# Local attention and two expert layers: larger loads for the mixed units, one load for the coarse values, a mask product in four tiles, and a new order

## The chip, the cores and the metric

The kernel runs on one core of one Trainium2 chip. The metric is the time of one execution on the device, in microseconds (us). Engines: PE is TensorE's matmul, PEld its weight load, DVE is VectorE, ACT is ScalarE, POOL is GpSimd, SP is SyncE, which here only issues DMAs.

## The reference

Three stages follow each other, all in float32 outside and at float32's precision inside.

- Attention: 2 batches, 8 heads, 576 positions, head size 64. Each position attends to the 7 positions at a distance under 4 (the local part). Beside it queries, keys and values are averaged over groups of four positions, 144 groups attend to all 144, and each result is repeated four times (the coarse part). The two results are added.
- First expert layer: h = x @ w_in with x of 1152 tokens x 512, w_in 512 x 2048; g = P(h)/Q(h), P a cubic with coefficients a, Q made of |h|, h squared and b; then g @ w_out back to 512.
- Second expert layer: the same shapes with g = h * tanh(log(1 + exp(h))).

The weights arrive as 64-bit words and are taken apart on the chip.

## The kernel before, in words

**Attention in units.** Heads are taken in pairs; 64-row halves of a tile hold the two heads of a pair. A unit is four windows of 64 queries. Kinds 0 and 1 are the four windows of one pair (tokens 0 to 255 and 256 to 511 of a batch). Kind 2 is the mixed unit: the last 64 tokens of all four pairs at once. There are 18 units, two of them mixed. prep() fetches and turns the keys of a pair, and sums its coarse values: load() at lines 551 to 561, vload() at 605 to 609 (a load of 64 rows and one of 8), then two additions at 615 and 619 on GpSimd or VectorE. unit() does one unit: qload() fetches queries (643; four loads in a mixed unit), vload() fetches window values (658; four loads, eight in a mixed unit), pe_a() transposes queries (546), pe_b() computes scores: first a product of eye2 and mask puts the mask in PSUM (702), then the local scores (709) and the coarse ones (717) are added on tiles of 64 rows by 32 columns. Maxima, exponentials and sums follow on VectorE and ScalarE, pe_d() transposes the weights (786, 791), pe_e() forms the coarse products (816) and the local ones (826).

**Expert layers.** A weight grain (256 columns of w_in or 256 rows of w_out) is fetched by load() at 983 and 988, and turned into a high and a low part by ScalarE and VectorE (lines 1000 to 1031). Each product is three: high x high, high x low, low x high (1144 and 1277 in the first layer; 1458, 1514 and 1279 in the second). In the second layer some products use seven in place of eight block products, with additions on VectorE (1480) between them, and sums() (1307 on) forms their inputs.

**Order.** Nothing runs in the order of the code. Each piece is a task with engines, an estimated cost, a due time (prio), buffers it takes and uses, and tasks it must follow. Plan.run() (114) walks through estimated time and issues on every engine the ready task with the smallest due time. It keeps an estimate of DMA too: up to 8 loads on their way, each with an issue time and a moving time. The due times are made from a step's place in the expert layers and constants: LEAD (attention ahead of its products), LLEAD and CLEAD (fetching and converting weights), LOFF, KOFF, VOFF, VROFF (loads of queries, keys, window values, coarse values against their unit), UOFF (one number per unit), GOFF (one per weight grain), SUMS. Where TensorE would have nothing, fill() puts in a product of a blank tile (line 527). All DMAs go out on SP's queue. Buffers of attention lie in one tile, "att", among them three places for queries, two for window values and one for coarse values, with more places in "wrk" for the first token group.

Of the kernel before, what the change touches and what calls it, by code (L numbers as in the profile page):

```python
# [12 lines left out]
BF16 = mybir.dt.bfloat16  # L13
# [7 lines left out]
NEG = -1.0e9  # L21
# [2 lines left out]
EDGE, LEAST = 2.0 ** -60, 1e-30  # L24


SECOND = 1.8
COLD, FILL_ALL = 3.4, 20
WINDOW, FILL, FILL_END = 3.4, 0.9, 450.0
LEAD, CLEAD, LLEAD, OLAG = 38, 14, 40, 18  # L30
PROL, PSTEP, VOFF, VROFF, LOFF, KOFF = -45, 2.5, 2, -1, 7, 9
GROUPS = ([6, 6, 4], [4, 4, 4, 4])
KCUT, MIX = 4, (1, 4)
MKP = -45
NKN, NVW, NXT, NQN = 2, 2, 3, 3
XVR, XQN, XVW = 2, 0, 0
SUMS = 5
NRAW, NWT, NRING, NRING2 = 2, 2, 3, (2, 1)
LAT = {"pe": 0.2, "act": 0.16, "dve": 0.15, "pool": 0.15, "sp": 1.1}
QUEUED = 8  # L40
UOFF = [-3.0, 0.0, 0.0, 3.0, 4.5, 3.0, 3.0, -1.5, 6.0, 0.0, 0.0, -4.5, -4.5, 4.5, 6.0, 4.5, -1.5, -1.5]
GOFF = [0.0, 0.0, 0.0, 0.0, -4.0, -4.0, -10.0, -6.0, 2.0, -4.0, 10.0, 12.0]
HP = 15


# [34 lines left out]
class Plan:  # L80
# [33 lines left out]
    def run(self, names):  # L114
# [79 lines left out]
        while True:  # L194
            for e in names:
# [3 lines left out]
                while ready[e]:  # L199
                    item = heapq.heappop(ready[e])  # L200
                    t = item[2]
                    if t.started:
                        continue
                    one = next(iter(t.engs))
                    if e != one and until[one] + t.engs[one] <= now + t.engs[e] + SECOND:
                        held.append(item)
                        continue
                    if not place(t, e):
                        held.append(item)
                        continue  # L210
                    t.started = True
                    t.fn(e) if len(t.engs) > 1 else t.fn()
                    begin = max(now, 0.65) if e == "sp" else now
                    if e == "pool" or e == "dve" and t.port:

                        begin = max(now, port[0])
                        port[0] = begin + t.engs[e]
                    end = until[e] = begin + t.engs[e] * (2 if e == "pe" and now < COLD else 1)
                    there = end + LAT[e]
                    if t.dma:  # L220
                        end = begin
                        for issue, move in t.dma:
                            end = max(end, landed[-QUEUED]) + issue
                            moved = max(moved, end + 0.3) + move
                            landed.append(moved + LAT["sp"])
                        until[e], there = end, landed[-1]
                    n += 1
                    heapq.heappush(events, (end, n, 0, e, t))
                    heapq.heappush(events, (there, n, 1, e, t))
                    for k in banks(t):  # L230
                        touched.setdefault(k, {})[e] = there
                    if t.next is not None:
                        t.next.deps -= 1
                        if not t.next.deps:
# [38 lines left out]
def kernel(  # L273
# [31 lines left out]


    ident = const.tile([128, 128], F32, name="ident")
    eye2 = const.tile([128, 128], BF16, name="eye2")
    mask = const.tile([128, 11, WK], BF16, name="mask")
    band = const.tile([64, 92], BF16, name="band")  # L310
# [54 lines left out]
    kn_s = lay("att", NKN, 768, parts=96)  # L365
    vr_s = lay("att", 1, 1024, (4, 4, D), parts=72)
    qn_s = lay("att", NQN, 256)
    vw_s = lay("att", NVW, 512, (4, 2, D), parts=64 + WK)
    s_s = lay("att", 2, 256, (4, 64))
    pd_s = lay("att", 2, SD)  # L370
# [78 lines left out]


    def bands():
        nc.gpsimd.affine_select(
            out=band, in_=band, compare_op=ALU.is_ge, fill=NEG, base=-8, pattern=[[1, 92]], channel_multiplier=-1,
        )
        nc.gpsimd.affine_select(
            out=band, in_=band, compare_op=ALU.is_ge, fill=NEG, base=14, pattern=[[-1, 92]], channel_multiplier=1,
        )

    def masks(kind, w, n):
        for b in range(2):  # L460
            h = slice(HB * b, HB * b + HB)
            lo = window(kind, w, b) - 64 * w + 11
            m0 = MASK0[kind] + (SLOT[w] if kind == 0 else 0)
            nc.vector.tensor_copy(
# [6 lines left out]

    def eyes():
        for h in range(2):
            nc.vector.tensor_copy(out=eye2[:64, 64 * h:64 * h + 64], in_=ident[:64, :64])
# [11 lines left out]
    def under():  # L486
        nc.vector.memset(eye2[64:], 0.0)
        nc.vector.memset(mask[64:], 0.0)

    t_m = add({"dve": 0.1}, lambda: nc.vector.memset(band, 0.0), -1900)  # L490
    t_un = add({"dve": 0.4}, under, -880)
    t_cd = add({"dve": 0.6}, zeros, -1000)
    t_bn = add({"pool": 0.5}, bands, -900, after=[t_m])
    t_mk = [
        add({"dve": 0.2 + 0.05 * len(ws)}, lambda x=(i, ws): [masks(x[0], *w) for w in x[1]], (-890, MKP, MKP)[i], after=[t_bn])
        for i, ws in enumerate((((0, 1), (1, 1), (2, 1), (3, 1)), ((4, 4),), ((8, 4),)))
    ]
# [50 lines left out]
    def prep(bb, p, prio, slots, start):  # L548
# [62 lines left out]
        m0 = add({"sp": 1.25}, vload, prio + VROFF, take=[vr], chain="vr", dma=[(0.65, 0.8), (0.6, 0.12)])  # L611

        def va(e):
            tv = vr.v
# [14 lines left out]
    def unit(u, slots, start):  # L629
# [4 lines left out]
        qn, vw, qp, qT, qx = Buf(qn_s + xq), Buf(vw_s + xv), Buf(slots["q"]), Buf(qT_s), Buf(qx_s)  # L634
        sc, pt, po, px = Buf(slots["s"]), Buf(slots["pt"]), Buf(slots["po"]), Buf(px_s)
        tm, s, pd, pT, od, xt = Buf(tm_s), Buf(s_s), Buf(pd_s), Buf(pT_s), Buf(od_s), Buf(xt_s)
        mix = [qx] if mixed else []

        def qload():
            for i, p in enumerate(pairs):  # L640
                w, m = wins[i][1], n // len(pairs)
                src = q[bb, 2 * p:2 * p + 2, 64 * w:64 * w + 2 * m, :]
                nc.sync.dma_start(  # L643
                    out=qn.v[m * i:m * i + m].rearrange("p (r h d) -> p r h d", h=2, d=D),
                    in_=src.rearrange("h (p r) d -> p r h d", r=2),
                )

        l0 = add({"sp": 0.65}, qload, prio - LOFF, take=[qn], chain="ld", dma=[(0.65, 0.24)] * 4 if mixed else [(0.65, 0.58)])

        m0 = MASK0[kind]  # L650
        keys = [(p, [window(kind, w, b) for b in range(2)]) for p, w in wins]

        def vload():
            for w0, nb in ((0, 4), (2, 4)) if not mixed else [(w, 2) for w in range(4)]:
                p, (k0, k1) = keys[w0]
                for hh in range(2):
                    src = v[bb, 2 * p + hh]
                    nc.sync.dma_start(
                        out=vw.v[64 * (w0 // 2):64 * (w0 // 2) + WK, 2 * (w0 % 2):2 * (w0 % 2) + nb, hh, :],
                        in_=bass.AP(src.tensor, src.offset + k0 * D, [[D, WK], [(k1 - k0) * D, nb], [1, D]]),  # L660
                    )

        vl = add({"sp": 1.0}, vload, prio + VOFF, take=[vw], chain="vw", dma=[(0.45, 0.11)] * 8 if mixed else [(0.45, 0.33)] * 4)

        def pe_a():
            q2 = qp.v[:, :2 * n].rearrange("c (p r) -> c p r", r=2)
            for r in range(2):
                flip(q2[:, :, r], qn.v, r, n)
# [30 lines left out]
        def pe_b():  # L699

            hs = [slice(0, 64), slice(64, 128)]
            nc.tensor.matmul(
                sc.v[:, :nw * WK], eye2, mask[:, m0:m0 + nw].rearrange("p w x -> p (w x)"), start=True, stop=False,
            )
            for w in range(nw):
                for b in range(2):
                    for h in hs:
# [12 lines left out]
                        )  # L720

        tb = add(
            {"pe": 1.6 if mixed else 0.86}, pe_b, prio,
            after=tq + [kv_done[p] for p in pairs] + [t_i16, t_un, t_mk[kind]],
            take=[sc, tm, s, pd],
            use=[qT] + mix, chain="pb",
        )
# [81 lines left out]
        def pe_e():  # L809
# [10 lines left out]
            for m in range(2):  # L820
                for b in range(2):
                    for hh in range(2):
                        for a in range(2):
                            h, r = hs[hh ^ a], slice(64 * a, 64 * a + WK)
                            c = 128 * m + h.start + HB * b
                            nc.tensor.matmul(  # L826
                                px.v[h, a, 64 * m + HB * b:64 * m + HB * b + HB], vw.v[r, 2 * m + b, hh ^ a, :],
                                pT.v[r, c:c + HB], start=True, stop=True,
                            )

# [603 lines left out]
    def seven(st):  # L1434
# [42 lines left out]
        def plus(dst, i, src, after, and_=None):  # L1477
# [96 lines left out]
```

## Time and profile before

| what | value |
|---|---|
| median of 3 runs | 482.44 us (480.46 to 484.45) |
| the profiled execution | 482.31 us, of which 480.4 us are the span from the first to the last instruction |
| granted TensorE clock | 0.998 |
| PE busy | 469.4 us, 98% |
| PEld busy | 429.1 us, 89% |
| DVE busy | 377.0 us, 78% |
| ACT busy | 338.3 us, 70% |
| POOL busy | 57.1 us, 12% |
| moved by DMA | 47.18 MB in 45981 packets, 30576 of them under 512 B |

Busy time is the time in which at least one instruction of the engine runs. Matmuls overlap, so a sum of their durations is more than the time they take on the engine. "Idle before" is the time an engine stood still before an instruction, with what released it. SPq is the queue of SP, in which a DMA's issue takes the time shown.

### The profile page before, as it was taken

What the parts mean: (1) busy time and instruction counts of PE and PEld (TensorE: products, weight loads), DVE (VectorE), ACT (ScalarE), POOL (GpSimd) and SP (SyncE); (2) the same over time, 40 slices, a digit from 0 to 9 for tenths busy, and PEclk for the clock granted to TensorE, in tenths of its full rate; (3) what the DMA queues carried; (4) which work ended last, traced back from release to release, by engine and by line L of the source; (5) the groups of instructions that cost most, each with busy time, mean ns of one, the idle gap of its engine ahead of it and who ended that gap; (6) DMA issues with size and microseconds to landing.
All of it is one profiled execution on the core that took longest, in us unless ns stands there. A gap on an engine that the chain in (4) does not pass through costs nothing.

```text
span 480.4 us, 9823 instructions
## 1 busy us (share of the span) xinstructions
PE 469.4 (98%) x4052; PEld 429.1 (89%) x4052; DVE 377.0 (78%) x565; ACT 338.3 (70%) x529; POOL 57.1 (12%) x80
## 2 busy tenths in 40 slices
PE   8998999999999999999999999999999999999996
PEld 4667888889999999999999999898989898989885
DVE  6677999899899968997998999988596669524342
ACT  5678898786889799998879797578666446422320
POOL 2644434563000000000000000000000000000000
PEclk9999999999999999999999999999999999999999
DMA  9878887611522312343022022134304220000103
GB/s 170 196 178 198 243 200 188 166 37 35 176 89 88 123 54 89 96 125 131 0 89 88 1 88 89 39 111 146 143 15 162 87 89 1 1 0 0 67 0 132
DMA packets 45981, 47.18 MB, mean 98 GB/s; under 512 B 30576, under 2 KB 31344, under 8 KB 45936
## 3 DMA queue, kind: packets, MB, share of 16 engines
q1 hardware_dynamic: 45936, 46.54, 33.7%
q8 instruction: 32, 0.52, 0.5%
q14 instruction: 13, 0.11, 0.1%
HBM read 44.17 MB, written 2.36 MB: 97 GB/s over the span
## 4 chain that ended last, share of the span: by engine, by line
PE 73%; DVE 13%; DMA 8%; ACT 3%; SPq 2%; issue 1%; ACTq 0%
PE psum L1279 19%; PE psum L1144 18%; PE psum L1277 15%; PE psum L1458 11%; PE psum L1514 5%; DMA att<-in_q_dram 3%; DMA raw<-in_moe_w_in_dram 3%; DVE wt L1014 1%; PE psum L826 1%; DMA att<-in_v_dram 1%; DVE xl L1300 1%; PE psum L546 1%; SPq L643 1%; DVE wrk L1318 1%; DVE wo L1031 1%
## 5 line engine op out<-in xcount | busy, mean ns | idle before, releaser
L1144 PE MATMUL psum<-xh,wi 128*128 128x384 f32 (+1 forms) x336 | 83.4, 319 | 0.2 <-DVE wrk L1173 0.2
L1277 PE MATMUL psum<-gg,wo 128*128 128x384 f32 (+1 forms) x480 | 76.3, 313 | 0.0
L1277 PEld LDWEIGHTS psum<-gg,wo 128*128 128x128 f32 x480 | 72.8, 189 | 0.4 <-issue 0.2
L1144 PEld LDWEIGHTS psum<-xh,wi 128*128 128x128 f32 x336 | 59.1, 189 | 1.4 <-issue 0.9
L1144 PE MATMUL psum<-xl,wi 128*128 128x384 f32 (+1 forms) x168 | 52.4, 312 | 0.0
L1279 PE MATMUL psum<-wo,gg 128*128 128x512 f32 x216 | 51.7, 391 | 0.0
L1279 PE MATMUL psum<-wo,late_g 128*128 128x512 f32 x216 | 51.3, 391 | 0.0
L1279 PEld LDWEIGHTS psum<-wo,late_g 128*128 128x128 f32 x216 | 40.4, 188 | 8.0
L1279 PEld LDWEIGHTS psum<-wo,gg 128*128 128x128 f32 x216 | 40.4, 188 | 7.9
L1014 DVE SCALAR_TENSOR_TENSOR wt<-wt,raw 128x1024 int32<-128x1024 int32 x32 | 40.0, 1252 | 6.8 <-ACT wt L1000 6.5
L1000 ACT ACTIVATE wt<-raw 128x1024 f32<-128x1024 f32 x32 | 36.5, 1140 | 10.9 <-DVE wo L1031 4.8
L1007 ACT ACTIVATE raw<-raw 128x1024 int32<-128x1024 uint16 x32 | 36.7, 1147 | 5.1 <-DMA raw<-in_moe_w_out_dram 3.4
L1514 PE MATMUL psum<-xh,wi 128*128 128x384 f32 x128 | 34.5, 335 | 0.0
L1144 PEld LDWEIGHTS psum<-xl,wi 128*128 128x128 f32 x168 | 31.8, 189 | 0.0
L1390 DVE TENSOR_TENSOR part<-psum,part 128x512 f32<-128x512 f32 x27 | 17.8, 687 | 13.7 <-PE psum L1279 13.7
L1144 PE MATMUL psum<-xh,late_r 128*128 128x384 f32 x96 | 25.5, 334 | 0.0
L527 PE MATMUL psum<-blank 128*128 128x480 bf16 x86 | 22.9, 390 | 1.2 <-DVE band L490 1.2
L1031 DVE TENSOR_TENSOR wo<-wt,wo 128x1024 fp32r<-128x1024 f32 x14 | 17.1, 1219 | 8.7 <-ACT wo L1026 8.7
L1026 ACT ACTIVATE wo<-wt 128x1024 fp32r<-128x1024 f32 x11 | 11.7, 1062 | 17.1 <-DVE wt L1020 7.7
L1514 PEld LDWEIGHTS psum<-xh,wi 128*128 128x128 f32 x128 | 23.3, 188 | 0.2
L1164 ACT ACTIVATE wrk<-psum 128x768 f32<-128x768 f32 (+1 forms) x27 | 19.8, 734 | 5.1 <-PE psum L1144 4.8
L1088 ACT ACT_TABLE_LOAD x17 | 21.8, 1283 | 0.3
(165 smaller groups left out, 1043.5 us busy)
## 6 DMA issues: line engine op xcount, KB each, us to landing
raw<-in_moe_w_in_dram SPq DMA_DIRECT2D x16, 1024.0 KB, 6.0
raw<-in_moe_w_out_dram SPq DMA_DIRECT2D x16, 1024.0 KB
att<-in_v_dram SPq DMA_DIRECT2D x64, 48.0 KB, 4.0
out_dram<-part SPq DMA_DIRECT2D x9, 256.0 KB, 2.1
att<-in_q_dram SPq DMA_DIRECT2D x16, 128.0 KB, 4.2
att<-in_k_dram SPq DMA_DIRECT2D x6, 288.0 KB, 4.5
att<-in_v_dram SPq DMA_DIRECT2D x6, 256.0 KB, 5.7
wrk<-in_k_dram SPq DMA_DIRECT2D x2, 288.0 KB
```

Of the source, the lines that this page charges most:

```text
L527: nc.tensor.matmul(view[:, :480], blank[:, :128], blank, start=True, stop=True)
L1000: nc.scalar.activation(out=t.v, in_=words(r)[:, :, 1].bitcast(F32), func=AF.Prelu if fold else AF.Identity, scale=2.0 ** -112, **({"alpha" ...
L1007: nc.scalar.activation(out=words(r)[:, :, 0], in_=r.v.bitcast(U16).rearrange("p (n four) -> p n four", four=4)[:, :, 1], func=AF.Copy, sca ...
L1014: nc.vector.scalar_tensor_tensor(out=ti, in0=ti, scalar=3, in1=words(r)[:, :, 0], op0=ALU.logical_shift_left, op1=ALU.bitwise_or)
L1031: ENG[e].tensor_tensor(out=w.v[:, 1], in0=s.v, in1=w.v[:, 0].bitcast(F32), op=ALU.subtract)
L1088: nc.scalar.preload_act_table_set(name)
L1144: nc.tensor.matmul(st.h.v[:, i, :T], w.v[:, ww, ks], xx[:, kk, c0:c0 + T], start=(nn == 0 and (st.big or i == 0)), stop=(nn == 3 * KD - 1 ...
L1164: nc.scalar.activation(out=vw(st.a), in_=H(), func=AF.Square)
L1277: nc.tensor.matmul(A(d)[:, :T], w.v[:, ww, lo + d * 128:lo + (d + 1) * 128], vw(gg)[:, i, :], start=start, stop=stop)
L1279: nc.tensor.matmul(A(d), vw(gg)[:, i, sl], w.v[:, ww, lo:lo + DM], start=start, stop=stop)
L1458: nc.tensor.matmul(dst.v[:, :TW], wv.v[:, ww, at:at + 128], x(h, kk), start=bool(take) and nn == 0, stop=nn == 5, skip_group_check=not take,)
L1514: nc.tensor.matmul(h.v[:, i, :TW], w.v[:, ww, at:at + 128], xx[:, kk, c0:c0 + TW], start=nn == 0, stop=nn == 3 * KD - 1)
```

## The change

- A mixed unit fetches its queries in one load of 64 rows by 8 heads (it was four loads), into a place of 512 columns that covers the last two of the three query places, and transposes four blocks of 64 rows in place of two of 128. Its window values come in four loads of four windows (eight of two), with another order of the windows in the tile.
- Coarse values come in one load of 72 rows.
- The mask product becomes four, on tiles of 64 rows by 32 columns; so eye2 has 64 columns on both halves, band and mask are filled on all 128 rows, and the two memsets of the lower halves go.
- The loads of a and b go out on ScalarE's queue, ahead of everything else there.
- The planner adds 0.8 us to its estimate of DMA for each 7 us that DMA moves (FETCH: packets that bring instructions).
- Constants of the order change; plus() of the second layer gets a due time earlier by HP.

```diff
-SECOND = 1.8
+SECOND = 1.6
-LEAD, CLEAD, LLEAD, OLAG = 38, 14, 40, 18
-PROL, PSTEP, VOFF, VROFF, LOFF, KOFF = -45, 2.5, 2, -1, 7, 9
+LEAD, CLEAD, LLEAD, OLAG = 38, 20, 30, 22
+PROL, PSTEP, VOFF, VROFF, LOFF, KOFF = -45, 2.5, 2, 2, 5, 9
-SUMS = 5
+SUMS = 20
-UOFF = [-3.0, 0.0, 0.0, 3.0, 4.5, 3.0, 3.0, -1.5, 6.0, 0.0, 0.0, -4.5, -4.5, 4.5, 6.0, 4.5, -1.5, -1.5]
-GOFF = [0.0, 0.0, 0.0, 0.0, -4.0, -4.0, -10.0, -6.0, 2.0, -4.0, 10.0, 12.0]
+FETCH = (0.8, 7.0)
+UOFF = [1.5, 0.0, 1.5, 12.0, 13.5, 13.5, 9.0, 18.0, 12.0, 9.0, -3.0, -6.0, -1.5, -3.0, 7.5, 10.5, -1.5, -9.0]
+GOFF = [0.0, 2.0, 0.0, 2.0, -4.0, -4.0, -4.0, -20.0, 18.0, 0.0, -6.0, 22.0]
...
-                            moved = max(moved, end + 0.3) + move
+                            first = max(moved, end + 0.3)
+                            moved = first + move + FETCH[0] * (int((first + move) / FETCH[1]) - int(first / FETCH[1]))
...
+    qm_s = [Place("att", qn_s[-2].lo, 512, (8, D), 64)]
...
-        for b in range(2):
-            h = slice(HB * b, HB * b + HB)
+        for r0 in range(0, 128, HB):
+            b, h = r0 // HB % 2, slice(r0, r0 + HB)
...
-        nc.sync.dma_start(out=a_sb, in_=a.partition_broadcast(128))
-        nc.sync.dma_start(out=b_sb, in_=b.partition_broadcast(128))
+        nc.scalar.dma_start(out=a_sb, in_=a.partition_broadcast(128))
+        nc.scalar.dma_start(out=b_sb, in_=b.partition_broadcast(128))
...
-    t_ab = add({"sp": 0.9}, c_sp, -34, dma=[(0.65, 0.1), (0.5, 0.1)])
+    t_ab = add({"act": 1.15}, c_sp, -2000, dma=[(0.65, 0.1), (0.5, 0.1)])
...
-            for lo, hi in ((0, 64), (64, 72)):
-                nc.sync.dma_start(out=dst[lo:hi], in_=src[lo:hi])
+            nc.sync.dma_start(out=dst, in_=src)
...
+            if mixed:
+                nc.sync.dma_start(out=qn.v, in_=q[bb, :, 64 * w:64 * w + 64].rearrange("h s d -> s h d"))
...
+            for a in range(2):
+                p, ks = keys[2 * a]
+                for i in range(2):
+                    src = v[bb, 2 * p + (0 if mixed else i)]
+                    k0, far = (ks[i], S) if mixed else (ks[0], ks[1] - ks[0])
...
-            nc.tensor.matmul(
-                sc.v[:, :nw * WK], eye2, mask[:, m0:m0 + nw].rearrange("p w x -> p (w x)"), start=True, stop=False,
-            )
+            for b in range(2):
+                for h in hs:
+                    r0 = h.start + HB * b
+                    nc.tensor.matmul(
+                        sc.v[r0:r0 + HB, :nw * WK], eye2[h, HB * b:HB * b + HB],
+                        mask[h, m0:m0 + nw].rearrange("p w x -> p (w x)"), start=True, stop=False, tile_position=(h.start, r0),
+                    )
...
-            return add({"dve": t_dve(TW)}, fn, pr, after=after, use=[src, dst])
+            return add({"dve": t_dve(TW)}, fn, pr - HP, after=after, use=[src, dst])
```

## Rows read from the trace of the kernel before

**Rows 1.** The line of cores: span, mean granted clock.

```profile
core 0: 480.4 us, clock 0.998
```

**Rows 2.** Stretches: length, busy (instructions) of PE, PEld, DVE, ACT, POOL; PEclk, DMA, GB/s.

```profile
8.00:43.00 35.00, 31.75 (x652) 21.62 (x650) 25.11 (x72) 26.43 (x73) 19.46 (x27) 1.00 0.88 196
43.00:65.00 22.00, 21.49 (x396) 19.32 (x398) 18.79 (x40) 18.97 (x44) 9.06 (x11) 1.00 0.72 191
65.00:80.00 15.00, 15.00 (x269) 12.82 (x267) 14.85 (x28) 13.51 (x34) 7.83 (x9) 1.00 0.87 187
80.00:115.00 35.00, 33.45 (x676) 29.48 (x676) 32.06 (x73) 27.07 (x69) 17.03 (x21) 1.00 0.47 118
115.00:310.00 195.00, 194.36 (x1210) 192.19 (x1209) 179.86 (x202) 164.53 (x196) 2.49 (x4) 1.00 0.25 82
310.00:475.00 165.00, 165.00 (x826) 149.07 (x825) 99.50 (x124) 84.44 (x114) 0.00 (x0) 1.00 0.20 68
```

**Rows 3.** The same view for line 527 on PE alone.

```profile
8.00:43.00 35.00, 12.44 (x50) 1.00 0.88 196
65.00:80.00 15.00, 3.67 (x14) 1.00 0.87 187
```

**Rows 4.** PE's waits: line, releaser, us in total, times, longest.

```profile
PE psum L546 <- DMA att<-in_q_dram: 2.8, 3, 1.6
PE psum L816 <- POOL att L619: 1.1, 2, 0.7
PE psum L826 <- DMA att<-in_v_dram: 0.9, 2, 0.6
PE psum L1458 <- DVE wrk L1480: 0.6, 1, 0.6
```

**Rows 5.** The chain that ended last, 0 to 45 us: start, length, what.

```profile
3.86 5.33 DMA att<-in_q_dram
9.67 1.42 PE psum L527 x7
19.27 6.06 DMA att<-in_q_dram
37.96 5.14 DMA att<-in_q_dram
```

**Rows 6.** SP's queue in order of time: start, length, line, what.

```profile
27.37 0.49 SPq L481 DMA_DIRECT2D a_sb<-in_moe_a_dram  x1
27.90 0.43 SPq L482 DMA_DIRECT2D b_sb<-in_moe_b_dram  x1
35.94 2.62 SPq L643 DMA_DIRECT2D att<-in_q_dram  x4
52.11 8.60 SPq L658 DMA_DIRECT2D att<-in_v_dram  x8
```

**Rows 7.** Lines 609 and 643: issue ns min/median/max; for 643 also time to landing.

```profile
L609 SPq DMA_DIRECT2D att<-in_v_dram x12: 487/568/987, 2.6 to 91.8; - x12
...
L643 SPq DMA_DIRECT2D att<-in_q_dram x24: 579/618/1191, 1.2 to 90.3; - x24
DMA to landing us min/median/max: 2.2/4.2/6.0
```

**Rows 8.** PE in order of time around a mask product; line 702 after 43 us.

```profile
14.65 0.25 PE L702 MATMUL psum<-mask,eye 128*128 128x192 bf16 x1
14.83 0.54 PE L709 MATMUL psum<-att 64*32 64x48 f32 x32
15.19 0.42 PE L717 MATMUL psum<-att 64*32 64x144 f32 x8
...
43.00:120.00 77.00, 2.54 (x10) 1.00 0.59 145
```

**Rows 9.** Mask copies on DVE; ACT's first work in order of time.

```profile
L464 DVE COPY mask<-band x12: 159/168/201, 2.8 to 5.0; 32x48 bf16<-32x48 bf16 x8, 32x192 bf16<-32x192 bf16 x4
...
5.89 1.74 ACT L587 ACTIVATE att<-psum 64x288 f32<-64x288 f32 x4 [3.87 <-PE psum L546]
```

**Rows 10.** SP's waits at the query loads.

```profile
SPq L643 <- PE psum L546: 1.3, 3, 0.6
```

More of the change, by code (lines that the diff above doesn't have):

```diff
@@ L307 @@
     ident = const.tile([128, 128], F32, name="ident")
-    eye2 = const.tile([128, 128], BF16, name="eye2")
+    eye2 = const.tile([128, 64], BF16, name="eye2")
     mask = const.tile([128, 11, WK], BF16, name="mask")
-    band = const.tile([64, 92], BF16, name="band")
+    band = const.tile([128, 92], BF16, name="band")
     blank = const.tile([128, 480], BF16, name="blank")
@@ L451, in bands @@
     def bands():
-        nc.gpsimd.affine_select(
-            out=band, in_=band, compare_op=ALU.is_ge, fill=NEG, base=-8, pattern=[[1, 92]], channel_multiplier=-1,
-        )
-        nc.gpsimd.affine_select(
-            out=band, in_=band, compare_op=ALU.is_ge, fill=NEG, base=14, pattern=[[-1, 92]], channel_multiplier=1,
-        )
+        for h in (slice(0, 64), slice(64, 128)):
+            nc.gpsimd.affine_select(
+                out=band[h], in_=band[h], compare_op=ALU.is_ge, fill=NEG, base=-8, pattern=[[1, 92]], channel_multiplier=-1,
+            )
+            nc.gpsimd.affine_select(
+                out=band[h], in_=band[h], compare_op=ALU.is_ge, fill=NEG, base=14, pattern=[[-1, 92]], channel_multiplier=1,
+            )
     def masks(kind, w, n):
-        for b in range(2):
-            h = slice(HB * b, HB * b + HB)
+        for r0 in range(0, 128, HB):
+            b, h = r0 // HB % 2, slice(r0, r0 + HB)
             lo = window(kind, w, b) - 64 * w + 11
@@ L473, in eyes @@
         for h in range(2):
-            nc.vector.tensor_copy(out=eye2[:64, 64 * h:64 * h + 64], in_=ident[:64, :64])
+            nc.vector.tensor_copy(out=eye2[64 * h:64 * h + 64], in_=ident[64 * h:64 * h + 64, 64 * h:64 * h + 64])
     def biases():
@@ L480, in c_sp @@
     def c_sp():
-        nc.sync.dma_start(out=a_sb, in_=a.partition_broadcast(128))
-        nc.sync.dma_start(out=b_sb, in_=b.partition_broadcast(128))
+        nc.scalar.dma_start(out=a_sb, in_=a.partition_broadcast(128))
+        nc.scalar.dma_start(out=b_sb, in_=b.partition_broadcast(128))
     add({"act": 1.3}, lambda: nc.scalar.preload_act_table_set("natural_log_exp_and_others"), -1000)
     t_id = add({"pool": 1.1}, lambda: make_identity(nc, ident), -1000)
-    def under():
-        nc.vector.memset(eye2[64:], 0.0)
-        nc.vector.memset(mask[64:], 0.0)
     t_m = add({"dve": 0.1}, lambda: nc.vector.memset(band, 0.0), -1900)
-    t_un = add({"dve": 0.4}, under, -880)
     t_cd = add({"dve": 0.6}, zeros, -1000)
-    t_bn = add({"pool": 0.5}, bands, -900, after=[t_m])
+    t_bn = add({"pool": 1.0}, bands, -900, after=[t_m])
     t_mk = [
-        add({"dve": 0.2 + 0.05 * len(ws)}, lambda x=(i, ws): [masks(x[0], *w) for w in x[1]], (-890, MKP, MKP)[i], after=[t_bn])
+        add({"dve": 0.4 + 0.1 * len(ws)}, lambda x=(i, ws): [masks(x[0], *w) for w in x[1]], (-890, MKP, MKP)[i], after=[t_bn])
         for i, ws in enumerate((((0, 1), (1, 1), (2, 1), (3, 1)), ((4, 4),), ((8, 4),)))
@@ L607, in vload @@
             dst = vr.v.rearrange("p (h t) f d -> p h (t f d)", h=2)
-            for lo, hi in ((0, 64), (64, 72)):
-                nc.sync.dma_start(out=dst[lo:hi], in_=src[lo:hi])
-        m0 = add({"sp": 1.25}, vload, prio + VROFF, take=[vr], chain="vr", dma=[(0.65, 0.8), (0.6, 0.12)])
+            nc.sync.dma_start(out=dst, in_=src)
+        m0 = add({"sp": 0.65}, vload, prio + VROFF, take=[vr], chain="vr", dma=[(0.65, 1.0)])
         def va(e):
@@ L633, in unit @@
         xq, xv = (wide_s["qn"], wide_s["vw"]) if start else ([], [])
-        qn, vw, qp, qT, qx = Buf(qn_s + xq), Buf(vw_s + xv), Buf(slots["q"]), Buf(qT_s), Buf(qx_s)
+        qn, vw, qp, qT, qx = Buf(qm_s if mixed else qn_s + xq), Buf(vw_s + xv), Buf(slots["q"]), Buf(qT_s), Buf(qx_s)
         sc, pt, po, px = Buf(slots["s"]), Buf(slots["pt"]), Buf(slots["po"]), Buf(px_s)
@@ L639, in qload @@
         def qload():
-            for i, p in enumerate(pairs):
-                w, m = wins[i][1], n // len(pairs)
-                src = q[bb, 2 * p:2 * p + 2, 64 * w:64 * w + 2 * m, :]
+            w = wins[0][1]
+            if mixed:
+                nc.sync.dma_start(out=qn.v, in_=q[bb, :, 64 * w:64 * w + 64].rearrange("h s d -> s h d"))
+            else:
                 nc.sync.dma_start(
-                    out=qn.v[m * i:m * i + m].rearrange("p (r h d) -> p r h d", h=2, d=D),
-                    in_=src.rearrange("h (p r) d -> p r h d", r=2),
+                    out=qn.v.rearrange("p (r h d) -> p r h d", h=2, d=D),
+                    in_=q[bb, 2 * pairs[0]:2 * pairs[0] + 2, 64 * w:64 * w + 2 * n].rearrange("h (p r) d -> p r h d", r=2),
                 )
-        l0 = add({"sp": 0.65}, qload, prio - LOFF, take=[qn], chain="ld", dma=[(0.65, 0.24)] * 4 if mixed else [(0.65, 0.58)])
+        l0 = add({"sp": 0.65}, qload, prio - LOFF, take=[qn], chain="ld", dma=[(0.45 if mixed else 0.65, 0.58)])
         m0 = MASK0[kind]
@@ L653, in vload @@
         def vload():
[L654 to L657, printed above, removed]
+            for a in range(2):
[3 more added lines that the diff above has]
+                    k0, far = (ks[i], S) if mixed else (ks[0], ks[1] - ks[0])
+                    here = vw.v[64 * a:64 * a + WK]
                     nc.sync.dma_start(
-                        out=vw.v[64 * (w0 // 2):64 * (w0 // 2) + WK, 2 * (w0 % 2):2 * (w0 % 2) + nb, hh, :],
-                        in_=bass.AP(src.tensor, src.offset + k0 * D, [[D, WK], [(k1 - k0) * D, nb], [1, D]]),
+                        out=here[:, 2 * i:2 * i + 2].rearrange("k w h d -> k (w h) d") if mixed else here[:, :, i],
+                        in_=bass.AP(src.tensor, src.offset + k0 * D, [[D, WK], [far * D, 4], [1, D]]),
                     )
-        vl = add({"sp": 1.0}, vload, prio + VOFF, take=[vw], chain="vw", dma=[(0.45, 0.11)] * 8 if mixed else [(0.45, 0.33)] * 4)
+        vl = add({"sp": 1.0}, vload, prio + VOFF, take=[vw], chain="vw", dma=[(0.45, 0.33)] * 4)
         def pe_a():
+            if mixed:
+                for i in range(nw):
+                    nc.tensor.transpose(
+                        qp.v[:, 64 * i:64 * i + 64], qn.v[:, 2 * i:2 * i + 2].rearrange("s h d -> s (h d)"), ident[:64, :64],
+                    )
+                return
             q2 = qp.v[:, :2 * n].rearrange("c (p r) -> c p r", r=2)
@@ L701, in pe_b @@
             hs = [slice(0, 64), slice(64, 128)]
-            nc.tensor.matmul(
-                sc.v[:, :nw * WK], eye2, mask[:, m0:m0 + nw].rearrange("p w x -> p (w x)"), start=True, stop=False,
-            )
+            for b in range(2):
[4 more added lines that the diff above has]
+                        mask[h, m0:m0 + nw].rearrange("p w x -> p (w x)"), start=True, stop=False, tile_position=(h.start, r0),
+                    )
             for w in range(nw):
@@ L722, in unit @@
         tb = add(
-            {"pe": 1.6 if mixed else 0.86}, pe_b, prio,
-            after=tq + [kv_done[p] for p in pairs] + [t_i16, t_un, t_mk[kind]],
+            {"pe": 1.52 if mixed else 0.78}, pe_b, prio,
+            after=tq + [kv_done[p] for p in pairs] + [t_i16, t_mk[kind]],
             take=[sc, tm, s, pd],
@@ L826, in pe_e @@
                             nc.tensor.matmul(
-                                px.v[h, a, 64 * m + HB * b:64 * m + HB * b + HB], vw.v[r, 2 * m + b, hh ^ a, :],
+                                px.v[h, a, 64 * m + HB * b:64 * m + HB * b + HB], vw.v[r, 2 * b + m if mixed else 2 * m + b, hh ^ a, :],
                                 pT.v[r, c:c + HB], start=True, stop=True,
```

## The prediction

> **What bounds the kernel now.** The first view is the line of cores: span 480.4 us at a granted clock of 0.998 [rows 1], so TensorE runs at the upper of its two levels and its clock leaves nothing to win. The profiled execution took 482.31 us, 1.9 more than its span and 0.13 below the median of the runs shown (482.44); the sum is made against 482.31.
>
> Then the busy time by stretch [rows 2]. From 115 to 475 us TensorE is busy without a gap but for 0.64 us (194.36 of 195, then 165.00 of 165), with the real work of the two expert layers. Nothing that happens earlier can shorten those 360 us except by letting them begin sooner. So the place to look is before 115 us, and there "busy" deceives: part of it is products of a blank tile (line 527), which the planner puts in where TensorE would wait. The same stretches for that line alone [rows 3] show 50 of them between 8 and 43 us and 14 between 65 and 80. Their busy time overlaps (390 ns of one, but seven begin within 1.42 us in a row of the chain [rows 5], so 0.20 us each): 10.0 and 2.8 us are waiting in disguise. Open idle comes on top, by length less busy [rows 2]: 3.25, 0.51, 0 and 1.55 us in the four stretches from 8 to 115. In all 18 us of lost TensorE time can be reached.
>
> What ends that waiting is a load: queries 2.8 us in three waits, window values 0.9, coarse values through GpSimd 1.1 [rows 4]. The chain up to 45 us runs through query loads of 5.33, 6.06 and 5.14 us [rows 5]. All of them go out on SP's queue, one after another, and DMA itself is 88% busy from 8 to 43 us [rows 2]. Either SP's issuing or the 16 engines behind it set the pace; the two give different results for this change.
>
> **Part A, fewer issues on SP.** Gone before the load at 37.96 are: the eight-row tail of four coarse loads, at 0.57 us each [rows 7], 2.3 us; the loads of a and b, 0.49 + 0.43 [rows 6], 0.92 us; three of the four query loads of the first unit of four pairs (2.62 us for four [rows 6], 0.62 each [rows 7]), 1.9 us. Together 5.1 us of issue time ahead of the last of these four, for which TensorE waits until 43.1 us [rows 5]. That is the upper end. The lower end is 0: the bytes and the pieces of 256 bytes stay as they are, and 88% of engine time leaves only 12% of 35 us, 4.2 us, to be saved by issuing sooner. I take the middle, 2.5 us. It can all be used, since 13 us of the stretch are filler and idle.
>
> At the coarse loads a view and a rule differ. By the view, the load moves the same bytes in one issue, and I count no price for its shape. The Trainium skill, "DMA: Bandwidth & Descriptors", section "Why a DMA increments its semaphore by 16 and not by 1", says a load is spread over the largest number up to 16 that divides its outer dimensions: 72 rows would get 12 engines, where 64 got 16 and 8 got 8. No row here shows the engines of one load, so this stands as a rival below.
>
> **Part B, window values of the mixed units, eight loads to four.** Eight took 8.60 us at 52 us [rows 6]; half is 4.3 us of SP. The stretch 43 to 65 has no filler and 0.51 us of idle: the first-layer products cover it. The second mixed unit's come after 92 us, where fewer than half of the DMA engines' time is used [rows 2]. I take 0; the ends are 0 and 0.5, the idle that there is.
>
> **Part C, the mask product in four.** One product over the whole array, 0.18 us until the next begins (14.65 to 14.83 [rows 8]), becomes four on quarters. The nearest row is the score products on such tiles, 32 in 0.36 us up to the next line [rows 8], 11 ns apart. Four of them take 45 ns to begin, and the blank product of the same type, 480 columns in 0.20 us, gives 0.08 for 192 columns: about 0.12, a gain of 0.06. Ten of the 18 run after 43 us [rows 8], where TensorE is filled: 0.6 us. The ends are 0.1 us a unit either way, 1.0 us in all, since no row shows such a product on quarters.
>
> **Set-up.** The band needs two selections more on GpSimd, the mask twelve more copies at 168 ns [rows 9], 2.0 us on VectorE, less two memsets. The last copy begins at 5.0 us now, and the keys that the first scores need leave ScalarE between 5.89 and 7.63 [rows 9]; two of the three kinds of mask may wait longer. I take 0, and up to 0.5 us lost if the cover is gone. The loads of a and b go ahead of ScalarE's table load; ScalarE idles 3.87 us before its first copy at 5.89 [rows 9], so their 0.92 us are hidden; on the DMA engines their 3 KB now meet the first loads of keys, for which I count nothing.
>
> **Part D, the new order.** Weights are fetched later and converted sooner, units are shifted by up to 19.5 us of due time, query loads become due 2 us and coarse loads 3 us later against their unit, the sums of the last layer are put off and the addition of line 1480 gets precedence. The last has an address: TensorE's wait of 0.64 us at 308 [rows 4] ends on that line. The rest can reach the filler of 65 to 80 (2.8) and the idle of 43 to 115 (2.1), 4.9 us. VectorE is 99% busy in 65 to 80 and 92% in 80 to 115 and 115 to 310 [rows 2], so an order that asks conversions sooner can also lose as much. I take 0.6 for the first and 1.9, two fifths, for the second: 2.5 us, with ends of +5.5 and -4.9.
>
> **Sum.** 2.5 + 0 + 0.6 + 2.5 = 5.6 us; 482.3 - 5.6 = 476.7 us. All parts at their good ends (5.1, 0.5, 1.0, 5.5) give 12.1, 470.2.
>
> **Rivals.**
> (1) The engines behind SP are the bound, so the merged loads give nothing, and the order gives only the addition of line 1480: 0.6 + 0.6 = 1.2, 481.1 us. For it: DMA is 88, 72 and 87% busy from 8 to 80 us [rows 2], and the packets are the same. Against it: the query loads of the chain [rows 5] were issued 5 to 6 us before TensorE wanted them, as soon as SP came to them.
>
> (2) Slower, by a buffer. The merged query load takes the last two of the three query slots at once, where four small loads needed one. SP's queue is in order; if one of the slots still holds another unit's queries, SP stands at this load and everything behind it, keys, window values and weights, stands too. Now SP hardly waits there: 1.3 us in three times [rows 10]. The price is one landing, 4.2 us in the median [rows 7], for each of the two mixed units, 8.4 us, against the gains of C and D, 3.1: 487.6 us. It decides from the point where SP's stop outlasts the ready products; at 43 to 65 us there is no filler left to give back.
>
> (3) The coarse load is uneven. If the 72 rows go to 12 engines, each of these moves 12 pieces of 2 KB, where the fullest eight moved 8 + 2. Per engine the stretch 8 to 43 shows 196 GB/s / 0.88 / 16 = 13.9 GB/s [rows 2], 0.15 us a piece, so 0.3 us more a load, 1.2 us for the four before 43 us: 477.9 us, just within 1%. The coarse values already hold up TensorE twice (1.1 us), which speaks for it; that the pieces are the largest of the attention loads, and so run faster than this mean, speaks against. By the rule of the page named above this is what happens.
>
> **The numbers.** What a measurement of this kernel can tell from no change is about 1%, 4.8 us: faster is below 477.6, slower above 487.3. The forecast has 0.45, with its own range from 470 to 477.6; rival 1 0.24, rival 3 0.13, rival 2 0.18. The first counts as faster, rivals 1 and 3 as within 1%, rival 2 as slower: 0.45, 0.37, 0.18. Their times lie from 470.2 to 487.6; with the bad ends of D and of the set-up beside rival 2 left out, and some room below for an order that also fills the first 8 us, the range is 469 to 488.
>
> **What would show it.** Part A: fewer blank products between 8 and 43 us (50 now), the first query waits at about 8.7 in place of 9.2, the load of the mixed queries landing near 40 in place of 43. If SP's gaps close but DMA's share goes above 0.9 and the fillers stay, rival 1 holds. Rival 2 would show as waits of SP at the query load's line on the transposes, rival 3 as coarse loads that keep some engines busy longer than others, and longer waits of the coarse products (1.1 us now). C: less than 0.18 us between a unit's mask product and its score products. D: no wait at line 1458 near 308, and fewer than 14 blank products in 65 to 80. The prediction is wrong if a gap opens after 115 us, where there is only the one of 0.64 now, or if the attention's last unit comes later than the products of the last token group want it.

## The result, and the profile after

The changed kernel takes 484.1 us in the median of 18 runs, the kernel before 481.55 us in 18 beside it: a ratio of 1.0053, 95% interval 1.0038 to 1.0067. It is slower by 2.5 us, where 5.6 us less were forecast. The profiled execution took 484.18 us with a span of 482.4 at a clock of 0.999.

The stretches of the changed kernel, with the columns of [rows 2]:

```profile
8.00:43.00 35.00, 34.97 (x660) 23.71 (x659) 24.37 (x68) 26.10 (x72) 17.47 (x26) 1.00 0.89 205
43.00:65.00 22.00, 22.00 (x439) 18.92 (x438) 20.31 (x43) 19.35 (x45) 8.81 (x9) 1.00 0.89 202
65.00:80.00 15.00, 14.44 (x240) 13.08 (x239) 13.99 (x27) 12.73 (x30) 7.33 (x9) 1.00 0.66 194
80.00:115.00 35.00, 35.00 (x670) 29.54 (x670) 31.82 (x68) 27.81 (x65) 16.98 (x22) 1.00 0.38 90
115.00:310.00 195.00, 194.98 (x1279) 192.03 (x1276) 179.10 (x205) 165.53 (x200) 5.02 (x5) 1.00 0.25 83
310.00:475.00 165.00, 164.53 (x825) 148.69 (x825) 101.00 (x127) 85.26 (x115) 0.00 (x0) 1.00 0.20 67
```

The blank products alone (line 526 now), to set beside [rows 3]:

```profile
8.00:43.00 35.00, 16.30 (x72) 1.00 0.89 205
43.00:65.00 22.00, 1.71 (x6) 1.00 0.89 202
65.00:80.00 15.00, 1.15 (x4) 1.00 0.66 194
80.00:115.00 35.00, 4.70 (x19) 1.00 0.38 90
```

All of TensorE's waits that its waiting view names, to set beside [rows 4]:

```profile
PE psum L526 <- DVE band L490: 1.2, 1, 1.2
PE psum L545 <- ACT att L682: 0.6, 1, 0.6
PE psum L1469 <- DVE wrk L1491: 0.5, 1, 0.5
```

No wait for a load is left; 2.8 us on queries, 0.9 on window values and 1.1 on coarse values are gone. But 31 blank products have come in (117 for 86): 22 more between 8 and 43 us, 6 more from 43 to 65, 18 more from 80 to 115, 10 fewer from 65 to 80 (one that crosses a border counts in both stretches). Their busy time grew by 7.6 us (22.88 to 30.47 over the span), TensorE's open idle, the span less the busy time, shrank by 4.9 (10.96 to 6.08). The share of "busy" rose from 98 to 99% while the kernel became slower.

A mask product and what follows it, for [rows 8]:

```profile
28.43 0.26 PE L712 MATMUL psum<-mask,eye 64*32 64x192 bf16 x4
28.52 0.51 PE L720 MATMUL psum<-att 64*32 64x48 f32 x32
28.86 0.41 PE L728 MATMUL psum<-att 64*32 64x144 f32 x8
```

Four products now take 0.09 us until the scores begin, where one took 0.18; that holds in 17 of the 18 units (in the first one 0.27 us pass), 1.4 us in all. So 7.6 - 4.9 - 1.4 = 1.3 of the 2.0 us by which the span grew are placed; the other 0.7 lie in many small differences that I can't place. Past 115 us nothing new opens. Attention ends later; its last products, first in the kernel before, then in the changed one:

```profile
120.26 0.67 PE L826 MATMUL psum<-att 48*64 48x32 f32 x32
```

```profile
124.69 0.67 PE L837 MATMUL psum<-att 48*64 48x32 f32 x32
```

### The profile page after: what moved, and what is told of

It reads as the page before. It is cut to its first block, busy times and chain, and to the rows that moved or that the text cites. A ratio compares the mean times of both kernels' runs of the same rounds, so it can differ in the third digit from the quotient of the medians.

```text
span 482.4 us, 9990 instructions
## 1 busy us (share of the span) xinstructions
PE 476.3 (99%) x4141; PEld 431.8 (90%) x4141; DVE 379.1 (79%) x574; ACT 339.5 (70%) x530; POOL 57.4 (12%) x82
## 2 busy tenths in 40 slices
DMA packets 45661, 47.17 MB, mean 98 GB/s; under 512 B 30256, under 2 KB 31024, under 8 KB 45616
## 4 chain that ended last, share of the span: by engine, by line
PE 86%; DVE 10%; ACT 3%; issue 1%; ACTq 0%
PE psum L1155 20%; PE psum L1290 18%; PE psum L1288 16%; PE psum L1469 11%; PE psum L526 6%; PE psum L1525 5%; PE psum L837 2%; PE psum L545 2%; PE psum L827 1%; PE psum L720 1%; PE psum L728 1%; DVE wt L1025 1%; PE psum L797 1%; PE psum L802 1%; DVE wt L1031 1%; DVE wrk L1329 1%
## 5 line engine op out<-in xcount | busy, mean ns | idle before, releaser
L526 PE MATMUL psum<-blank 128*128 128x480 bf16 x117 | 30.5, 393 | 1.2 <-DVE band L490 1.2
L526 PEld LDWEIGHTS <-blank 128*128 128x128 bf16 x117 | 11.4, 103 | 11.5 <-issue 3.6
```

The costliest lines, as they stand in the source:

```text
L526: nc.tensor.matmul(view[:, :480], blank[:, :128], blank, start=True, stop=True)
```

## The experiments

Each ratio is to runs of the kernel before on the same chip, so two experiments are best compared by their ratios. First the change was cut in two. **parts_only** has the loads and the mask product, with the old constants:

```diff
...
-LEAD, CLEAD, LLEAD, OLAG = 38, 20, 30, 22
+LEAD, CLEAD, LLEAD, OLAG = 38, 14, 40, 18
...
-FETCH = (0.8, 7.0)
+FETCH = (0.0, 7.0)
...
```

> The new loads, the four mask products and a and b on ScalarE's queue, but the old constants, the old due time of the additions and no DMA surcharge in the planner. Its program has 106 blank products, the changed kernel 117, the kernel before 86. Theory O (the new order costs, the parts gain): the mask products and shorter score lines give 1.5 to 2 us, the fewer issues 0 to 3: 0.5 to 1% faster than before, 476.5 to 479.5 us. Rival P (a part costs, for instance the coarse load of 72 rows or the query load over two slots): as slow as the changed kernel or slower, 483 to 486 us, with open waits of TensorE on coarse values or queries.

Measured: 484.34 us, 1.0068 (1.0044 to 1.0093). **order_only** has the new constants, the surcharge and the earlier additions on the old loads and the old mask product.

> The old loads and the old mask product with all new constants, the DMA surcharge and the earlier additions. Its program has 147 blank products, 61 more than before. Theory O: the new order is what costs; 3 to 8 us slower than before, 485 to 490 us, with hardly any open wait of TensorE. Rival P: the order is good by itself, 478 to 481 us.

Measured: 495.19 us, 1.0311 (1.0285 to 1.0337). parts_only is as slow as the whole within its interval, order_only is far slower. That refutes "the parts gain" in this form, but this cut is no cut: with other costs or constants the planner makes another order (106 and 147 blank products, where before and after have 86 and 117), so a part and a new order are measured together. Open waits on coarse values or queries, as rival P wants them, did not show in parts_only.

So the next runs hold an order fixed. The two **short** kernels keep their order and shorten the blank products after the first 20:

```diff
...
-        nc.tensor.matmul(view[:, :480], blank[:, :128], blank, start=True, stop=True)
+        warmed.append(1)
+        n = 480 if len(warmed) <= 20 else 128
+        nc.tensor.matmul(view[:, :n], blank[:, :128], blank[:, :n], start=True, stop=True)
```

> The changed kernel in the same order, but every blank product after the first 20 has 128 columns in place of 480 (it computes nothing that is used). About 97 of them shrink from 0.20 to some 0.06 us, 13 us of TensorE. Theory H (the order holds TensorE with blank products while the work behind them is ready): at least 5 us faster than the changed kernel, below 479 us, if the granted clock stays near 1. Rival L (the blank products only cover loads and vector work that are late): 0 to 2 us faster, 482 to 484 us, and the 13 us come back as open waits of TensorE.

> The kernel before with the same shortening: 66 blank products lose about 0.14 us each, 9 us. Theory H says that there they cover real waits, since open waits of 4.8 us stand beside them: 0 to 3 us faster, 478.5 to 481.5 us. Rival L says the same of both kernels, so the difference between this run and the shortened changed kernel stays 2 to 3 us.

Measured: after_short 481.79 us, 1.0015 (0.9993 to 1.0037); before_short 481.09 us, 0.9998 (0.9976 to 1.0021). Shortened, the changed kernel gets some 2 us back (1.8 by the ratios, 2.3 by the times) of the 13 estimated. The rest comes back as waiting: in the profiled execution of after_short (clock 0.999) TensorE is busy for 28.2 of the 35 us from 8 to 43, and these are four of its six largest waits (the others are the start and one that nothing in the profile releases):

```profile
PE psum L724 <- ACT att L686: 2.4, 4, 0.8
PE psum L549 <- ACT att L686: 1.3, 2, 0.9
...
PE psum L1292 <- DVE gg L1258: 1.0, 1, 1.0
PE psum L801 <- POOL att L785: 1.0, 2, 0.6
```

None of these is for a load. So in the new order theory H holds for a small part and rival L for the larger: most blank products stand where vector work is not ready. Rival L's other forecast failed: the two shortened kernels differ by 0.7 us, not by 2 to 3.

before_short says less, because its clock fell. Its profile page gives the granted clock in 40 slices, in tenths (9 is 90% or more):

```profile
PEclk9979999899999999999999999999999999999999
```

All 12 of its runs have a mean granted clock of 0.988 to 0.996, where 40 of the 103 runs of the kernel before beside these experiments are at 0.996 or below and the other 63 at 0.998 or above. What its shorter products gave, the lower clock may have taken, so it can't tell whether the blank products of the old order cover real waits. 8 of the 12 runs of after_short are at 0.996 or below too; the other four have a median of 481.2 us, so its reading stands.

Now the parts in the old order. **mask4_same** makes the mask product in four, **loads_same** merges coarse and window values, **mask_loads_same** does both; the planner's costs stay as they were, so all other instructions, and the 86 blank products, stand in the order of before. The edit of loads_same, in part:

```diff
-            for lo, hi in ((0, 64), (64, 72)):
-                nc.sync.dma_start(out=dst[lo:hi], in_=src[lo:hi])
+            nc.sync.dma_start(out=dst, in_=src)
...
-            for w0, nb in ((0, 4), (2, 4)) if not mixed else [(w, 2) for w in range(4)]:
...
+            for a in range(2):
+                p, ks = keys[2 * a]
...
```

> The kernel before with the mask product in four alone; the planner's costs are left as they were, so every other instruction stands in the order of before, with its 86 blank products. Theory M (the products on quarters are 0.09 us shorter a unit, and with the order held this is not given back): 10 units after 43 us, 0.9 us, up to 1.6 for all 18: ratio 0.997 to 0.998. Rival V (vector work paces the stretch before 115 us, so TensorE only waits longer): no change, 0.999 to 1.001.

> The kernel before with coarse values in one load of 72 rows and window values of mixed units in four, in the old order (planner's costs unchanged). 12 issues fewer on SP. If SP's issuing bounds the first 43 us, as I forecast: 1 to 2.3 us faster, 0.995 to 0.998, with shorter waits on queries. If the loads are not the bound (V): 0.999 to 1.001. If 72 rows in one load are slow: slower by 0.3 us a load, up to 1.005, with longer waits of the coarse products.

> Both parts of the two runs beside it, in the old order. If the parts are good and only the new order costs, this beats both kernels: 0.993 to 0.996, 478 to 479 us. Under V it equals the kernel before within 0.2%.

Measured: mask4_same 481.09 us, 0.9998 (0.9973 to 1.0024); loads_same 477.25 us, 0.9913 (0.9891 to 0.9936); mask_loads_same 479.72 us, 0.9962 (0.9936 to 0.9987). The loads are good, more than the 1 to 2.3 us forecast for them: 4.2 us from 16 issues (171 loads and stores become 155; the expectation counted 12, and 20 in place of 24 for all the loads further on). TensorE's waits in loads_same:

```profile
PE psum L527 <- DVE band L490: 1.2, 1, 1.2
PE psum L710 <- issue: 0.9, 1, 0.9
PE psum L827 <- issue: 0.8, 1, 0.8
PE psum L1459 <- DVE wrk L1481: 0.6, 1, 0.6
```

No wait on a load is named any more, as in the changed kernel, but without one blank product more; what ended the two of "issue" the profile does not show. mask_loads_same, with the same loads, still waits 1.0 us for queries. The stretch of loads_same from 8 to 43 us, and its last attention products:

```profile
8.00:43.00 35.00, 33.30 (x665) 23.32 (x664) 25.14 (x73) 27.30 (x74) 20.36 (x27) 1.00 0.93 207
```

```profile
116.70 0.67 PE L827 MATMUL psum<-att 48*64 48x32 f32 x32
```

The DMA engines were not full at a share of 0.88 [rows 2]; with fewer issues they reach 0.93 and 207 GB/s here, 0.90 and 202 in mask_loads_same. The attention ends 3.6 us sooner than before, where the changed kernel ends it 4.4 later. The mask product shows its 0.09 us in its two runs too, but the time does not tell it from nothing.

That mask_loads_same looks 2.5 us slower than loads_same on the same chip lies for the most part in the clock. All six runs of loads_same are at 0.998 or above, but only 5 of 12 of mask_loads_same, 8 of 12 of mask4_same and 18 of 29 of the kernel before. The medians of these alone are 477.3, 477.7, 480.8 and 480.8 us. So at the upper clock the loads gain 3.6 us, 3.1 with the mask product, and the mask product by itself nothing.

**short_dve** asks whether vector work was the bound of the old order (the join, line 1014, which puts a weight's bits together on VectorE, runs on 256 of 1024 columns of each weight grain of the first layer):

```diff
...
-            ti = t.v.bitcast(I32)
...
+            n = DM // 2 if first else 2 * DM
+            ti = t.v.bitcast(I32)[:, :n]
...
```

> The kernel before with shortened blank products (481.1 us) and VectorE relieved: the joining of the first layer's weights (16 instructions of 1.25 us) is done on a quarter of the columns, the rest of the weights stay unjoined. That takes about 0.9 us from each, some 9 us of VectorE before 115 us, and moves nothing else. Theory V (vector work, not loads, sets the pace before 115 us): 3 to 9 us faster than the shortened kernel, 472 to 478 us. Rival D (loads set the pace): 480 to 481.5 us, same as the shortened kernel.

Measured: 481.4 us, 0.9995 (0.9976 to 1.0014), the same as before_short. The time is that of rival D, and the first of its waits speaks for it:

```profile
PE psum L550 <- DMA att<-in_q_dram: 4.2, 2, 2.5
```

The test is weaker than it was meant to be. Only six of the sixteen joins of the first layer come before 115 us; there they take 4.5 us in place of 7.8, so 3.3 us of VectorE were taken away and not 9. And 11 of its 12 runs are at a clock of 0.996 or below, as all of before_short are. That vector work did not pace the old order is therefore likely, not shown.

**loads_all_same** adds the merged query load (into a place of its own) and puts a and b on ScalarE's queue; **loads_short** shortens the blank products of loads_same; **after_oldloads** is the changed kernel in its own order with the old number of loads (coarse values in two, window values of a mixed unit in eight, its queries in four, still into the wide place; a and b stay on ScalarE's queue); **after_nofetch** lets the planner work without the surcharge:

```diff
-FETCH = (0.8, 7.0)
+FETCH = (0.0, 7.0)
```

> The kernel before in its old order with all the loads of the change: coarse values in one, window values of mixed units in four, the mixed queries in one (into a place of their own, so that the order can stay), a and b on ScalarE's queue. 20 issues fewer on SP than before, 8 more than in loads_same left out. Theory A (issues on SP pace the first 43 us): a little faster than loads_same, 475 to 477 us, ratio 0.986 to 0.991. Rival: the open waits are gone already (2.4 us of idle left, 1.2 of them the start), so nothing more, 477 to 478 us.

> loads_same (477.3 us) with the blank products after the first 20 cut from 480 to 128 columns. Theory H (with the loads early, blank products now hold TensorE for nothing): 3 to 8 us faster than loads_same, 469 to 474 us. Rival L (they cover vector work that is late in any case): 0 to 1.5 us faster, 476 to 477.5 us, the rest comes back as open waits on ScalarE, VectorE and GpSimd.

> The changed kernel in its own order (planner's costs unchanged, 117 blank products), but with the loads as before: coarse values in two, window values of mixed units in eight, mixed queries in four. Theory G (the new order puts blank products where loads used to be waited for, so early loads buy nothing there): 0 to 1.5 us slower than the changed kernel, 484 to 485.5 us. Rival: the loads are worth 4 us there too, and the order alone costs 6 to 7: 487 to 489 us, with open waits on queries.

> The changed kernel without the DMA surcharge in the planner; all else is left, and the planner makes another order with 112 blank products (117 with it). If the surcharge is what makes the order late (rival F): 478 to 481 us. If it is the order as a whole, made anew with any cost that moves (theory O): 482 to 487 us, like the changed kernel.

Measured: loads_all_same 479.01 us, 0.9957 (0.9934 to 0.998); loads_short 478.26 us, 0.9935 (0.9909 to 0.9961); after_oldloads 484.11 us, 1.006 (1.0039 to 1.0082); after_nofetch 486.09 us, 1.0099 (1.0071 to 1.0127). The decisive one is after_oldloads: the same loads that are worth 2 to 4 us in the old order are worth nothing in the new one. With the eight loads and the tails back, 171 in all, TensorE still waits for no load (the interval of a difference of two such ratios is some 1.3 us either way):

```profile
PE psum L526 <- DVE band L490: 1.2, 1, 1.2
PE psum L1471 <- DVE wrk L1493: 0.5, 1, 0.5
```

The other three: more merging than in loads_same brings nothing more; it measures 0.44% less, and 2.2 us in place of 3.6 at a clock of 0.998 or above, against both forecasts. With the loads early the blank products are still no burden in the old order (477.2 us in the four of nine runs at that clock, 477.3 in loads_same). And the surcharge is not what makes the order slow, for without it the order has 112 blank products and is 2 us slower.

Two causes of the new order's price were then tried. **after_short_ownq** and **after_ownq** give the merged queries a place of their own, in the same order; **after_short_dve** relieves VectorE as above.

```diff
...
-                nc.sync.dma_start(out=qn.v, in_=q[bb, :, 64 * w:64 * w + 64].rearrange("h s d -> s h d"))
+                nc.sync.dma_start(out=q_mix_s.view, in_=q[bb, :, 64 * w:64 * w + 64].rearrange("h s d -> s h d"))
...
```

> The changed kernel with shortened blank products (481.8 us) and a place of its own for the merged queries, in the same order. SP stood at that load for 7.4 us in the changed kernel, waiting for the two query places. If that stop is what delays the attention behind it (rival 2 of the prediction): 2 to 6 us faster than the shortened changed kernel, 476 to 480 us. If the loads are early enough without it (theory G): 481 to 482.5 us, with SP's stop gone.

> The same with the blank products at full length. Theory G and the rival alike: 483.5 to 484.5 us, since TensorE's order with its 117 blank products leaves nothing to be won; below 482 us would say that the stop was felt through other waits.

> The changed kernel with shortened blank products and the join of the first layer's weights done on a quarter of the columns (the rest stays unjoined), some 9 us less of VectorE before 115 us. In the order of before this gave nothing, since the queries came late. Theory V2 (in the new order, with the loads early, vector work is what TensorE waits for): 3 to 8 us faster than the shortened changed kernel, 474 to 479 us. Rival (the order itself, not the length of any work, keeps products apart): 480 to 482.5 us.

Measured: after_short_ownq 481.26 us, 1.0022 (0.9994 to 1.0051); after_ownq 484.05 us, 1.0068 (1.0045 to 1.0092); after_short_dve 479.26 us, 0.997 (0.9943 to 0.9997). In the changed kernel SP did stand at the merged load, by its own waits:

```profile
SPq L640 <- PE psum L545: 7.4, 2, 6.2
```

This wait is gone in after_short_ownq, and the time stays: in this order the stop costs nothing that can be told. Relief of VectorE (2.7 us in place of 7.5 for the six joins before 115 us) brings 2.2 us by the ratios against after_short in the new order and 2.0 against after_short_ownq on the same chip. That is less than theory V2 asked, but from half the relief it counted on. The last view is of the changed kernel around 41 us, all engines in order of time:

```profile
40.57 0.38 PE L802 MATMUL psum<-ident,att 128*72 128x128 f32 x2
40.62 0.35 DVE L772 TENSOR_REDUCE att<-att 128x4 f32<-128x192 f32 x1
...
40.79 2.39 PE L526 MATMUL psum<-blank 128*128 128x480 bf16 x11
...
41.21 0.19 DVE L776 RECIPROCAL att<-att 128x5 f32<-128x5 f32 x1
...
41.57 0.51 POOL L781 TENSOR_TENSOR att<-att 128x192 f32<-128x192 f32 x1 [2.88 <-DVE att L776]
...
42.06 0.39 POOL L786 TENSOR_SCALAR att<-att 128x144 f32<-128x144 f32 x1
...
43.02 0.38 PE L797 MATMUL psum<-ident,att 128*112 128x128 f32 x2
```

Eleven blank products run while a unit's weights are normalized on VectorE and GpSimd; these end at 42.45, the transposes begin at 43.02. So some 1.7 us of the 2.2 are true waiting, and 0.6 are blank products longer than the wait. The order has put no products of the first layer there; whether any were ready is not shown.

## Why the prediction was wrong, point by point

**What bounds the kernel.** Right for the old order: queries, window values and coarse values ended the waits before 115 us, and taking the wait for them away makes the kernel faster (loads_same); relief of VectorE did not (short_dve), in a weaker test. It does not hold for the new order, in which no load is late even with the old loads.

**Part A**, 2.5 us forecast: right as a mechanism, in the old order. Coarse and window values alone, A's tails together with B's loads, gave 4.2 us (0.64 to 1.09%), all the loads together 2.1 (0.2 to 0.66%). So A's other two terms, the queries of the mixed units and a and b, 2.8 us of its 5.1, gave nothing that shows. The cap of 4.2 us from DMA's share was not passed. It is no firm one, since single stretches read more than 1 in this view (1.03 from 80 to 90 us of the kernel before). In the changed kernel the same step is worth 0.

**Part B**, taken as 0, was only measured together with the coarse loads, so it stays open.

**Part C**, 0.6 us: the product's time was sized a little short (0.09 gained a unit, 0.06 forecast), and the kernel's time shows neither that nor its absence (0.9973 to 1.0024).

**Part D is the step that failed.** I took +2.5 us with ends of +5.5 and -4.9; with the same loads the old order has a ratio of 0.9957, the new one of 1.0053. It costs about 5 us (4.6 by the ratios; 484.1 against 478.6 at a clock of 0.998 or above), the bad end; the new one has the mask product too, which showed nothing by itself. The error was to book two fifths of the filler and idle of the old order as a gain, with no row that shows what the new order would do with them, and to add that to the gains of the loads. An order is one thing: the new one takes away the waits that the loads would have shortened, and has 31 blank products elsewhere, so A was not there to be added. The term of D with an address, 0.6 us for the wait at the additions, gave 0.1: it is 0.5 us now. Why this order is slower stays open in part: shorter blank products give some 2 us back in it (after_short) and less vector work some 2 more (after_short_dve), each a difference of ratios with an interval of 1.3 to 1.7 us either way; these are remedies, and that the order lost its time there is not shown. Which of the constants brings it can't be told by turning one back, since that makes another order altogether.

**The rivals.** Rival 1 has the time nearest to the result (481.1) and the wrong reason, since the loads do gain; as a change from its base, rival 2 (+5.3) is nearer than rival 1 (-1.2). Rival 2 has its mechanism (SP's stop of 7.4 us) and no price; [rows 10] was also only a part, for before the change SP waited at that line 3.4 and 2.3 us more, until loads of weights had landed. Rival 3 has its condition and not its price. Its price: the 72-row load is issued in 0.31 to 0.51 us in loads_same, in place of two of 0.57; from the first issue to the last piece of the coarse values 5.5 us pass in the median, 5.6 before; and the waits of the coarse products, 1.1 us before, are gone. Its condition: by the rule of the Trainium skill, "DMA: Bandwidth & Descriptors", section "Why a DMA increments its semaphore by 16 and not by 1", 72 rows would use 12 engines. The trace agrees: each 72-row load of loads_same steps its semaphore once 0.5 to 0.7 us after its issue and twelve times after 2.9 us or more. Before, a 64-row load did so sixteen times, an 8-row one once early and eight times late.

The version to keep is the kernel before with merged coarse and window loads in the old order: 0.9913 (0.9891 to 0.9936) of the kernel before in six runs, faster than both.

## What to carry to other kernels

Where a program's order is made by a planner, measure a part with the order held: leave its costs as they were and change only what is emitted. Parts that together looked like a loss of 0.5% held a gain of 0.4 to 0.9%. And products that only fill time count as busy, so set them and the open idle side by side before and after; a wait that vanishes from the list of waits may have been replaced by them. Where kernels differ in how often their clock falls, set runs at the same granted clock side by side: so the 2.5 us between loads_same and mask_loads_same became 0.5.

## What the runs showed of the hardware

Fewer and larger loads raised the share and the rate of the DMA engines from 8 to 43 us: in the old order from 0.88 and 196 GB/s to 0.93 and 207 (0.90 and 202 in mask_loads_same, 0.96 and 210 with all merged), in the new one from 0.84 and 193 (after_oldloads) to 0.89 and 205. The bytes of the whole run stay the same, 47.18 and 47.17 MB.

A load of 72 rows ends in twelve late steps of its semaphore, one of 64 rows in sixteen and one of 8 rows in eight; over a load of these sizes no price of it shows (5.5 us to the last step in loads_same, 5.6 for the pair of loads before).

Shorter blank products cost clock. All runs of the changed kernel, of after_oldloads, after_ownq and after_nofetch have a mean granted clock of 0.998 or above; with most of the blank products cut to 128 columns, 8 of 12 runs of after_short and all 12 of before_short are at 0.996 or below. The number of blank products alone does not decide it, since order_only has 147 and fell in two of five runs. In the profiled execution of before_short TensorE was busy for 0.92 of the 3 us from 22 to 25; between 25 and 26 the clock fell to its lower level, 1.2 GHz, and between 32 and 33 it was back.
